# A new order of the opening, query sums on VectorE, and the shared group's sums on VectorE

## The chip, the cores and the metric

The kernel runs on one core of a Trainium2 chip. The metric is the device time of one execution in microseconds (us); lower is better. A core has a matrix engine (TensorE, PE in the profile), a vector engine (VectorE, DVE), a scalar engine (ScalarE, ACT), a general engine (GpSimd, POOL) and a queue engine that only issues transfers (SyncE, SP). Each engine takes its instructions in the order written, and waits on semaphores for the others.

## What is computed

The reference, cut to what matters (B, H, S, D of a head = 8, 8, 576, 64):

```python
# efficient attention, per batch and head
q_s = exp(q - max(q, axis=-1));  q_s = q_s / (sum(q_s, axis=-1) + 1e-9)   # over the 64 features
k_s = exp(k - max(k, axis=seq)); k_s = k_s / (sum(k_s, axis=seq) + 1e-9)  # over the 576 tokens
x = q_s @ (k_s^T @ v)                       # (8, 8, 576, 64), then heads side by side: (8, 576, 512)
# Fourier mix and channel block
u = x + real(fft(fft(x, axis=seq), axis=features))
un = (u - mean(u)) / sqrt(var(u) + 1e-6)
out = u + relu(un @ w_ch1) @ w_ch2          # 512 -> 2048 -> 512
```

All data are 32-bit floats, except that the two weights reach the device as 64-bit words, whose halves are turned into 32-bit floats there (`convert`).

## The kernel before

The eight batches are worked off as groups. For each batch the 576 tokens are taken as four tiles of 128 (A to D in the opening) and 64 left-over tokens; the left-over tokens of two batches share one tile `t`, whose results form an eighth group of 512 rows, the shared group. The groups run in the order 0 to 6, then the shared group, then 7 (`groups`). Group 0 uses plain products with the two weights (`plain`), converts the weights in passing (`convert`) and leaves seven Strassen combinations of their quarters in DRAM (`combine`, `deepen`). The later stages, numbered 1 to 8 by `order`, stream these and multiply by Strassen's scheme (`up`, `deep_down`), while attention and Fourier mix of the next batch go on beside them. Order 7 is the shared group's stage, with no attention beside it, and order 8 the last.

The order of all instructions is written out by hand: each step is a pair of a due time and a function; all pairs are sorted by time and called once, and the engines then follow this order. The due times set the order only, not the moment. The opening, which is all the work ahead of group 0's first up-projection, is a list of names and times in the string `OPENING`. In it:

- `loads_first` issues the loads. ScalarE's queue gets four loads of 32 rows of the shared tile (`shared`, L271); SP gets the four key loads (L281), two query loads of two tiles each (L290: A and B, then C and D), the values (L285, L286), the four first rows of the shared tile (`shared_firsts`, L274, which overwrite one row of each of ScalarE's four loads), tables, the second batch's keys and values, and the first weights (L347).
- `first_keys` turns keys to exponentials, transposes them (`turn`, `last`) and multiplies by the values (`kv`); `scale` writes the normalised matrix `kvr`.
- `q_exp_spread` gives the exponential of a query tile: a maximum on VectorE (`max`, L805), a subtraction (`less`, L810) on GpSimd, for the shared tile on VectorE, and an exponential on ScalarE (L814).
- `q_turn` transposes a query tile and copies it to a buffer `qT`, of which there are two.
- `q_times_kv` multiplies `qT` by a matrix of ones to get the sums of the exponentials (`ones`, L876), by `kvr` (`times`, L884), inverts the sums (`inverse`, L890 and L891) and scales the product on its way to the result tile `x` (`out`, L899). The shared tile takes its sums and scaling ahead of the transposition (`q_inverse`, L783 to L794, VectorE).
- `folded` adds and subtracts the four result tiles (`tokens`, L945) and folds columns, `block` and `mix_own` are the two steps of the Fourier transform, `norm` the statistics, scaling and transposition for the up-projection, whose first chunk is `half` (L1169) and whose others are `up` in `plain` (L1160).
- `c0` is the conversion of the first weight chunk; those of chunks 1 to 31 are placed by the list `words` behind the opening, whose end is the time `first`.

In `up`, `a_side` (L383 to L386) forms four sums of finished hidden blocks on the engine `e`. In `deep_down`, `a_step` (L1317) forms further sums, `into` (L1321) adds finished results to `x`, `sums` (L1324) adds results to each other; some of them run on the engine `E`. `plus` (L1378) adds a bank of products to an earlier one and so frees the bank for TensorE. For order 8, `e` and `E` are VectorE, otherwise GpSimd.

Results leave by `store`. Where rows have to be turned round (c not equal to u), the tile goes to DRAM (`mirror`, L1529) and from there in reversed order to the output (L1531). At the very end, `scatter` does it instead by an indirect store on GpSimd's queue (L1506) with a list of rows made by `iota`: once for half of a tile, once for a whole tile.

Of the kernel before, what the change touches and what calls it, by code (L numbers as in the profile page):

```python
# [40 lines left out]
F32 = mybir.dt.float32  # L41
I32, U32 = mybir.dt.int32, mybir.dt.uint32
# [4 lines left out]
P = 128  # L47
# [37 lines left out]
WARM = (3, 3), (24.7, 6), (41.9, 2), (43.45, 1), (44.5, 1)  # L85
OPENING = """
4.30 k00 max, 5.10 k00 exp, 5.50 k01 max, 6.05 k00 turn, 6.30 k01 exp, 6.65 k02 max, 7.06 k00 four,
7.25 k01 turn, 7.56 k02 exp, 7.75 k03 max, 8.32 k01 four, 8.51 k02 turn, 8.82 k03 exp, 8.90 A max, 9.50 B max,
9.58 k02 four, 9.65 A less, 9.77 k0 last, 10.10 k0 inverse, 10.27 k03 turn, 10.42 k0 fifth, 10.69 B less,
10.80 A exp, 11.20 k00 kv, 11.30 k03 four, 11.84 B exp, 11.85 A turn, 12.20 C max, 12.30 k01 kv, 12.45 A copy,  # L90
12.80 D max, 12.95 B turn, 12.95 C less, 13.40 A ones, 13.55 B copy, 13.99 D less, 14.10 C exp, 14.20 k02 kv,
14.35 A inverse, 14.85 C turn, 15.00 t max, 15.14 D exp, 15.30 k03 kv, 15.75 t less, 15.95 D turn,
16.35 k0 scale0, 16.40 B ones, 16.47 t exp, 16.80 k0 scale1, 17.14 t inverse, 17.25 B kv, 17.99 B inverse,
18.22 A kv, 18.35 C copy, 18.39 t normal, 19.01 B out, 19.19 t turn, 19.32 D copy, 19.63 k10 max, 19.69 C ones,
19.84 t copy, 20.30 A out, 20.43 k10 exp, 20.49 C kv, 20.92 C inverse, 21.39 t fold, 21.46 D ones,
22.09 t join, 22.26 D kv, 22.51 D inverse, 22.91 C out, 23.31 t kv, 23.53 D out, 24.15 tokens0, 24.21 k10 turn,
24.36 t parts, 24.77 tokens1, 25.39 columns0, 25.46 k10 four, 25.75 columns1, 26.23 by1, 26.59 by0,
26.80 c0 hi, 26.95 t folds, 27.45 c0 lo, 27.70 again0, 28.00 again1, 28.50 tokens3, 28.60 b0 times,
29.12 tokens2, 29.58 b1 times, 29.74 columns3, 29.80 b0 copies, 30.10 columns2, 30.56 b4 times, 30.58 by2,
30.78 b1 copies, 30.94 by3, 31.42 again2, 31.72 again3, 31.76 b4 copies, 32.22 k12 max, 32.32 b2 times,  # L100
32.89 c0 shift, 33.02 k12 exp, 33.30 b3 times, 33.59 c0 sign, 33.78 b2 copies, 34.19 k13 max, 34.28 k12 turn,
34.31 c0 add, 34.50 b3 copies, 34.86 k11 max, 35.05 k13 exp, 35.20 m0 times, 35.81 k12 four, 36.10 k13 turn,
36.31 m0 copy, 36.55 m1 times, 36.66 k11 exp, 36.81 m0 sums, 37.42 k13 four, 37.61 k1 last, 37.71 m0 add0,
37.92 m1 copy, 38.07 k11 turn, 38.27 k1 fifth, 38.39 m0 add1, 38.42 m1 sums, 38.77 k11 four, 38.92 k10 kv,
39.22 s00, 39.27 roots, 39.67 k11 kv, 39.69 m1 add1, 39.97 s01, 40.42 k12 kv, 40.87 root0, 40.99 m1 add0,
41.17 k13 kv, 41.67 scales0, 41.87 s11, 42.02 normal01, 42.62 s10, 42.77 turn01, 43.37 normal00, 43.52 root1,
43.87 scales1, 43.89 normal11, 43.95 laid01, 44.02 turn00, 44.22 normal10, 44.77 laid00, 44.87 turn10,
45.47 turn11, 45.62 laid10, 46.22 laid11, 53.00 k1 inverse, 53.30 k1 scale0, 53.60 k1 scale1"""
# [28 lines left out]
class _Block:  # L137
    def __init__(self, ctx, tc, q, kT, v, w1, w2, ft, cd, out):
# [38 lines left out]
        self.ones = c.tile([P, NR, H], F32, name="ones")  # L177
        nc.gpsimd.memset(self.ones[:], 0.0)
        for h in range(2):
            nc.gpsimd.memset(self.ones[64 * h:64 * h + 64].rearrange("p r h -> p (r h)")[:, h::H + 2], 1.0)  # L180

# [31 lines left out]
        self.unused = None  # L213
# [32 lines left out]
    def loads_first(self, fetch):  # L246
# [45 lines left out]
        def second(r):  # L292
# [6 lines left out]
        order = [lambda: nc.gpsimd.memset(v[0:64, 4, :], 0.0), shared, table, *(lambda r=r: keys(r) for r in range(NR)), lambda: queries(0),  # L299
                 lambda: values(0), lambda: queries(1), lambda: values(2), shared_firsts, self.tables,  # L300
# [214 lines left out]
    def first_keys(self, b):  # L515
# [4 lines left out]
        copy, box, top = nc.vector.tensor_copy if b == 0 else nc.scalar.copy, {}, {}  # L520
# [26 lines left out]
        def fifth():  # L547
            copy(self.fifth[64:], box["last"][64:])
# [26 lines left out]
    def opening(self, fetch, converted):  # L575
# [17 lines left out]
        named("t max,t less,t exp", self.q_exp_spread(shared, V))  # L593
        named("t inverse,t normal", self.q_inverse(shared, V, V))
# [3 lines left out]
        for n, it in own.items():  # L598
            named(f"{n} max,{n} less,{n} exp", self.q_exp_spread(it))
            named(f"{n} turn,{n} copy", self.q_turn(it))  # L600
            named(f"{n} ones,{n} kv,{n} inverse,{n} out", self.q_times_kv(it))
# [13 lines left out]
        for i in range(1):  # L615
            some = converted(i)
            named(f"c{i} hi,c{i} shift,c{i} sign,c{i} lo,c{i} add", some[:5])
            steps[f"c{i} add"] = lambda some=some: go(some[4:])
# [179 lines left out]
    def q_exp_spread(self, it, e=None):  # L798
# [9 lines left out]
        def less():  # L808
            m = live[it].pop()[:].unsqueeze(2).to_broadcast([P, H, DH])
            (e or nc.gpsimd).tensor_tensor(out=heads(), in0=heads(), in1=m, op=ALU.add)  # L810
# [14 lines left out]
    def q_turn(self, it):  # L825
# [3 lines left out]
        def copy():  # L829
            pt = box.pop()  # L830
            qT = self.work.tile([P, NR, P], F32, tag="qT", name="qT", bufs=2)
            self.nc.scalar.copy(qT[:], pt[:] if c == u else pt[:, :, ::-1])
# [34 lines left out]
    def q_times_kv(self, it):  # L867
# [3 lines left out]
        def ones():  # L871
# [813 lines left out]
```

## Time and profile before

| | us |
|---|---|
| median of 3 runs | 1072.61 (1072.57 to 1073.12) |
| profiled execution, its own time | 1072.76 |
| its span, first to last instruction | 1071.0 |
| TensorE busy | 1058.3 |
| VectorE busy | 685.9 |
| ScalarE busy | 404.8 |
| GpSimd busy | 422.5 |
| first up-projection product starts | 49.20 |
| last TensorE product ends | 1066.9 |

The granted TensorE clock is 0.999 over the span. The page gives the busy time of each engine, the span in slices, and the costliest groups of instructions by line, engine and operation, each with its count, its mean and the idle time ahead of it. In the timeline a row has start, duration, engine, line, operation, destination and source, shape, count, and in brackets how long the engine stood idle before and what released it. Rows of equal instructions in a run are merged: the duration is then that of all of them. A matrix product of 32-bit floats takes two passes on TensorE, and each pass is one MATMUL; a transposition takes one.

### The profile page before, as it was taken

The numbers are of one execution on the slowest core, as the hardware profiler recorded it, in microseconds if no ns is written. First come the engines' busy times: TensorE is split into PE (matmuls) and PEld (weight loads), VectorE is DVE, ScalarE is ACT, GpSimd is POOL, SyncE is SP. The second block draws the span as 40 slices with busy tenths as digits, with TensorE's granted clock in tenths as the row PEclk, the third lists the DMA queues.
The fourth block names the chain that finished last, engine by engine and source line by source line (L and its number), as shares of the span: only waits on it lengthen the run. The fifth ranks groups of instructions, "written<-read, shape, count | busy, mean of one in ns | idle before, by whom it ended". The sixth has DMA issues, their size and how long they took to land.

```text
span 1071.0 us, 16992 instructions
## 1 busy us (share of the span) xinstructions
PE 1058.3 (99%) x6394; PEld 922.4 (86%) x6394; DVE 685.9 (64%) x1317; ACT 404.8 (38%) x953; POOL 422.5 (39%) x352
## 2 busy tenths in 40 slices
PE   8999999999999999999999999999999999999998
PEld 7744556988898899889998999889988998899898
DVE  6897787684455874677556765687457742563563
ACT  5675534632245215521453234522552132131210
POOL 3262220265412743454515543374336353552000
PEclk9999999999999999999999999999999999999999
DMA  9486578648976576646755576547644674576464
GB/s 341 160 302 245 174 246 292 208 162 282 329 262 212 179 252 233 225 177 202 273 178 190 196 246 224 199 183 256 222 167 158 210 257 164 203 249 217 176 214 146
DMA packets 112933, 235.90 MB, mean 220 GB/s; under 512 B 22756, under 2 KB 74212, under 8 KB 102228
## 3 DMA queue, kind: packets, MB, share of 16 engines
q1 hardware_dynamic: 112244, 233.90, 63.8%
q8 instruction: 51, 0.84, 0.3%
q10 hardware_dynamic: 480, 0.52, 0.1%
q0 software_dynamic: 128, 0.39, 0.1%
q14 instruction: 30, 0.25, 0.1%
HBM read 199.66 MB, written 38.93 MB: 223 GB/s over the span
## 4 chain that ended last, share of the span: by engine, by line
PE 84%; DVE 3%; ACT 2%; issue 1%; POOL 1%; DMA 0%; POOLq 0%; DVEq 0%; ACTq 0%
PE bb L1244 15%; PE bb L1371 10%; PE bc L1244 10%; PE ba L1244 10%; PE bc L1371 6%; PE ba L1371 6%; PE bb L1341 4%; PE acc L716 2%; PE acc L884 2%; PE bc L1181 2%; PE bb L1460 2%; PE acc L997 2%; PE acc L1000 2%; PE acc L1025 2%; PE bc L1460 1%; PE ba L1460 1%
## 5 line engine op out<-in xcount | busy, mean ns | idle before, releaser
L1244 PE MATMUL bb<-unT,big 128*128 128x256 f32 x768 | 184.4, 380 | 0.8 <-DVE u L1214 0.8
L1244 PEld LDWEIGHTS bb<-unT,big 128*128 128x128 f32 x768 | 142.5, 190 | 20.3 <-DVE u L1214 2.3
L383 POOL TENSOR_TENSOR big<-big 128x512 f32<-128x512 f32 x28 | 35.9, 1281 | 255.9 <-ACT big L1256 255.9
L1256 ACT ACTIVATE big<-big 128x512 f32<-128x512 f32 x96 | 60.6, 631 | 194.9 <-DVE big L1255 194.5
L1244 PE MATMUL ba<-unT,big 128*128 128x256 f32 x512 | 123.8, 379 | 0.0
L1244 PE MATMUL bc<-unT,big 128*128 128x256 f32 x512 | 123.5, 380 | 0.0
L1214 DVE TENSOR_TENSOR u<-bb,s 128x512 f32<-128x512 f32 x66 | 45.6, 691 | 117.7 <-PE bb L1244 97.4
L1371 PE MATMUL bb<-big 128*128 128x128 f32 x848 | 105.2, 275 | 1.8 <-DVE u L1378 1.8
L1244 PEld LDWEIGHTS bc<-unT,big 128*128 128x128 f32 x512 | 94.7, 190 | 12.5 <-DVE big L1255 1.0
L1244 PEld LDWEIGHTS ba<-unT,big 128*128 128x128 f32 x512 | 94.4, 190 | 12.2 <-issue 0.5
L1371 PEld LDWEIGHTS bb<-big 128*128 128x128 f32 x848 | 99.6, 192 | 2.2 <-DVE u L1378 2.2
L1321 POOL TENSOR_TENSOR x<-x,big 128x512 f32<-128x512 f32 x45 | 57.7, 1297 | 62.7 <-issue 32.9
L1317 DVE TENSOR_TENSOR big<-big 128x512 f32<-128x512 f32 x94 | 78.1, 875 | 2.5 <-POOL big L386 2.5
L1371 PE MATMUL ba<-big 128*128 128x128 f32 x640 | 79.6, 275 | 0.0
L766 ACT ACTIVATE q<-q,qm 128x64 f32<-128x64 f32 x248 | 67.5, 342 | 31.2 <-DVE qm L760 25.9
L1371 PEld LDWEIGHTS ba<-big 128*128 128x128 f32 x640 | 76.3, 192 | 1.2
L1341 PE MATMUL bb<-big 128*128 128x256 f32 x256 | 58.7, 380 | 0.0
L1378 DVE TENSOR_TENSOR u<-bb,s 128x256 f32<-128x256 f32 x40 | 16.8, 421 | 64.6 <-PE bb L1371 59.9
L1255 DVE TENSOR_TENSOR big<-bc,u 128x512 f32<-128x512 f32 x64 | 44.0, 687 | 21.9 <-PE bc L1244 21.0
L1341 PEld LDWEIGHTS bb<-big 128*128 128x128 f32 x256 | 48.2, 190 | 8.0 <-DVE big L1255 1.1
L1371 PE MATMUL bc<-big 128*128 128x128 f32 x416 | 51.5, 275 | 0.0
L1371 PEld LDWEIGHTS bc<-big 128*128 128x128 f32 x416 | 48.9, 192 | 0.0
(265 smaller groups left out, 2014.8 us busy)
## 6 DMA issues: line engine op xcount, KB each, us to landing
big<-w2d SPq DMA_DIRECT2D x67, 1024.0 KB, 4.8
big<-w1s SPq DMA_DIRECT2D x64, 896.0 KB, 4.9
big<-w2s SPq DMA_DIRECT2D x16, 1024.0 KB, 6.4
big<-in_w_dram SPq DMA_DIRECT2D x21, 512.0 KB, 6.3
w2d<-big SPq DMA_DIRECT2D x42, 256.0 KB, 5.6
q<-in_q_dram SPq DMA_DIRECT2D x28, 256.0 KB, 6.4
k<-in_kT_dram SPq DMA_DIRECT2D x24, 288.0 KB, 5.6
v<-in_v_dram SPq DMA_DIRECT2D x24, 256.0 KB, 4.4
```

The lines of the kernel that those rows point to most:

```text
L383: e1.tensor_tensor(out=to(4), in0=at(2), in1=at(3), op=ALU.add)
L716: nc.tensor.matmul(pk, lhsT=ks[:, c, :], rhs=v[:, c, :], start=(c == 0), stop=(c == NC - 1))
L766: nc.scalar.activation(q[:, h, :], q[:, h, :], ACT.Exp, bias=m[:, h:h + 1])
L1214: plus = lambda t: V.tensor_tensor(out=temp(t), in0=box["bb"][:], in1=box["s1"][:], op=ALU.add)
L1244: nc.tensor.matmul(bank()[:, i, :], lhsT=w[:, WA_AT[m], k * P:(k + 1) * P], rhs=self.unT[g][:, B_AT[m], k, :], start=first and i == 0 and ...
L1255: steps = [(0, lambda: V.tensor_tensor(out=hp(i), in0=bank()[:], in1=u()[:], op=ALU.add)), (0.8, lambda: nc.scalar.activation(hp(i), hp(i) ...
L1256: (0.8, lambda: nc.scalar.activation(hp(i), hp(i), ACT.Relu))]
L1317: e.tensor_tensor(out=to(o), in0=to(x), in1=to(y), op=op)
L1321: E.tensor_tensor(out=x, in0=x, in1=tile(m), op=ALU.add)
L1341: nc.tensor.matmul(box[name][:, i, :], lhsT=h[p][:, A_AT[m], i * P:(i + 1) * P], rhs=self.stream[n][:, p, :], start=p == 0 and (m != 1 or ...
L1371: nc.tensor.matmul(box[place[n]][:, i, :], lhsT=own(m)(A_AT[n])[:, f, :], rhs=w[:, r // 2, r % 2 * P:r % 2 * P + P], start=first and f == ...
L1460: nc.tensor.matmul(bank()[:, i, :], lhsT=h[p][:, A_AT[m], i * P:(i + 1) * P], rhs=w[:, p, :], start=first and i == 0 and p == 0, stop=p == ...
```

## The change

The list `OPENING` is written anew, and with it:

- The sums of the four query tiles and of the shared tile are formed by VectorE (`reduce_sum`) as soon as the exponential is there, into one small tile `sums`; the matrix of ones and its products go. Two steps invert them, `inverse1` for the shared tile and C, `inverse2` for D, A and B.
- The shared tile, C and D are scaled on GpSimd ahead of their transposition; A and B are still scaled by VectorE on the way out of the product. C's and D's products are copied by ScalarE, and `tokens` reads them where they were formed.
- The shared tile's subtraction moves from VectorE to GpSimd, the fifth-row copy of the first keys (`fifth`) from VectorE to ScalarE.
- The transposed query tiles of batch 0 have a place each in the weight buffer `w1sb`, and three of the four products have a bank of their own.
- The load of the four first rows of the shared tile is issued ahead of the first query load.
- The second weight chunk's conversion (`c1`) moves into the opening; four warm-up products instead of three stand at its start; `first` is 47.6 instead of 46.9.
- `e` and `E` are VectorE for order 7 too.
- At the end the indirect store of half a tile becomes a store to DRAM and a mirrored one from there, both on SP.

```diff
-WARM = (3, 3), (24.7, 6), (41.9, 2), (43.45, 1), (44.5, 1)
+WARM = (3, 4), (23.6, 6), (42.1, 1), (43.9, 1)
...
-        order = [lambda: nc.gpsimd.memset(v[0:64, 4, :], 0.0), shared, table, *(lambda r=r: keys(r) for r in range(NR)), lambda: queries(0),
-                 lambda: values(0), lambda: queries(1), lambda: values(2), shared_firsts, self.tables,
+        order = [lambda: nc.gpsimd.memset(v[0:64, 4, :], 0.0), shared, table, *(lambda r=r: keys(r) for r in range(NR)), shared_firsts, lambda: queries(0),
+                 lambda: values(0), lambda: queries(1), lambda: values(2), self.tables,
...
-            copy(self.fifth[64:], box["last"][64:])
+            nc.scalar.copy(self.fifth[64:], box["last"][64:])
...
-        named("t max,t less,t exp", self.q_exp_spread(shared, V))
-        named("t inverse,t normal", self.q_inverse(shared, V, V))
+        named("t max,t less,t exp", self.q_exp_spread(shared))
+        sums = self.small.tile([P, 5, H], F32, tag="sums", name="sums", bufs=1)
+        firsts = {"t": shared, **{n: own[n] for n in "CDAB"}}
+        heads = {n: self.live[it][0].rearrange("p (h d) -> p h d", h=H) for n, it in firsts.items()}
+        spread = {n: sums[:, i].unsqueeze(2).to_broadcast([P, H, DH]) for i, n in enumerate(firsts)}
+        for i, n in enumerate(firsts):
+            steps[f"{n} sum"] = lambda i=i, n=n: V.reduce_sum(sums[:, i], heads[n], axis=AX.X)
+            if n in "tCD":
+                steps[f"{n} normal"] = lambda n=n: G.tensor_tensor(out=heads[n], in0=heads[n], in1=spread[n], op=ALU.mult)
+            else:
+                self.live[own[n]].append(spread[n])
+
+        def inverse(s):
+            V.tensor_scalar(out=sums[:, s], in0=sums[:, s], scalar1=ATT_EPS, scalar2=None, op0=ALU.add)
+            V.reciprocal(sums[:, s], sums[:, s])
+
+        for i, s in enumerate((slice(0, 2), slice(2, 5))):
+            steps[f"inverse{i + 1}"] = lambda s=s: inverse(s)
...
-            named(f"{n} ones,{n} kv,{n} inverse,{n} out", self.q_times_kv(it))
+            named(f"{n} kv,{n} out", self.q_times_kv(it))
...
-        for i in range(1):
+        for i in range(2):
             some = converted(i)
...
-            qT = self.work.tile([P, NR, P], F32, tag="qT", name="qT", bufs=2)
-            self.nc.scalar.copy(qT[:], pt[:] if c == u else pt[:, :, ::-1])
+            if b == 0:
+                qT = self.w1sb[:, 1 + c + 2 * u, :].rearrange("p (r n) -> p r n", n=P)
+            else:
+                qT = self.work.tile([P, NR, P], F32, tag="qT", name="qT", bufs=2)[:]
+            self.nc.scalar.copy(qT, pt[:] if c == u else pt[:, :, ::-1])
...
-            px = self.acc((P, D))
-            box.insert(0, px)
+            if b == 0 and (c, u) != (1, 0):
+                n = {(0, 0): "bb", (1, 1): "bc", (0, 1): "ba"}[c, u]
+                t = self.ps.tile([P, 512], F32, tag=n, name=n)
+                px = t[:]
+            else:
+                px = self.acc((P, D))
+            box.append(px)
             box.extend(rec)
+            if b == 0 and c != u and not rec:
+                self.px[c, u] = px
...
-        base, e = self.base[order], V if order == B else nc.gpsimd
+        base, e = self.base[order], V if order >= B - 1 else nc.gpsimd
...
-        E = V if last else G
+        E = V if order >= B - 1 else G
...
-            steps.extend(self.scatter(t - 8 + 3.1, g, 1, 0, lambda: self.xs[g, 0][:, 1, HD:], 1))
+            half(t - 8 + 3.1, 1, 0, 1, 3)
...
-    first, second, both = 46.9, 56, 77
+    first, second, both = 47.6, 56, 77
...
-    words = [first + 0.3, first + 1.4, *(first + 0.9 + 1.7 * i for i in range(1, NF - 2))]
+    words = [first + 0.7, *(first + 0.9 + 1.7 * i for i in range(1, NF - 2))]
...
-    for i, dt in enumerate(words, 1):
+    for i, dt in enumerate(words, 2):
```

## The prediction

> **What bounds the kernel now.** First the page's busy line, then the table of busy time by stretch (us, TensorE, its weight loads, VectorE, ScalarE, GpSimd, each with its number of instructions, then granted clock, DMA share, GB/s).
>
> ```profile
> PE 1058.3 (99%) x6394; PEld 922.4 (86%) x6394; DVE 685.9 (64%) x1317; ACT 404.8 (38%) x953; POOL 422.5 (39%) x352
> ```
> ```profile
> 0.00:24.00 24.00, 20.83 (x139) 18.55 (x140) 14.29 (x32) 13.54 (x26) 9.53 (x29) 1.00 0.98 336
> 24.00:49.20 25.20, 23.21 (x167) 20.63 (x167) 22.35 (x59) 15.10 (x40) 5.02 (x6) 1.00 0.62 213
> 876.00:972.00 96.00, 94.41 (x607) 87.61 (x607) 45.19 (x67) 22.96 (x39) 46.71 (x35) 1.00 0.63 218
> ```
>
> From 49.2 us on TensorE has hardly a pause, and the order and number of its products stay the same there. So only three places can change the time: when TensorE starts the first up-projection, the 1.6 us that it loses in the seventh stage (876 to 972), and what follows its last product. I read these three in the timeline, with the landing times of loads and stores beside it. The opening:
>
> ```profile
> 3.60 0.39 SPq L290 DMA_DIRECT2D big<-in_q_dram  x1
> 7.30 0.62 SPq L274 DMA_DIRECT2D big<-in_q_dram  x1
> 8.65 1.28 DVE L805 TENSOR_REDUCE qm<-big 128x8 f32<-128x512 f32 x2 [0.50 <-DMA big<-in_q_dram]
> 9.48 2.04 POOL L810 TENSOR_TENSOR big<-big,qm 128x512 f32<-128x512 f32 x2 [4.17 <-DVE qm L805]
> 26.14 1.28 DVE L945 TENSOR_TENSOR eo<-x 128x512 f32<-128x512 f32 x2
> 49.20 3.62 PE L1169 MATMUL ba<-unT,big 128*128 128x256 f32 x16
> 53.02 3.70 PE L1160 MATMUL bb<-unT,big 128*128 128x512 f32 x8 [0.19 <-POOL big L377]
> ```
>
> Read: the first query load is issued at 3.60 and releases VectorE's first query maximum at 8.65; the four-row load of the shared tile (L274) stands behind six larger loads; the first up-projection starts at 49.20, and the second chunk waits for GpSimd to finish its weight. The seventh stage:
>
> ```profile
> 926.13 1.58 POOL L383 TENSOR_TENSOR big<-big 128x512 f32<-128x512 f32 x1 [6.90 <-ACT big L1256]
> 931.14 1.26 POOL L386 TENSOR_TENSOR big<-big 128x512 f32<-128x512 f32 x1
> 932.44 5.68 DVE L1317 TENSOR_TENSOR big<-big 128x512 f32<-128x512 f32 x4 [2.50 <-POOL big L386]
> 938.04 0.41 DVE L1378 TENSOR_TENSOR u<-bb,s 128x256 f32<-128x256 f32 x1
> 938.51 2.05 PE L1371 MATMUL bb<-big 128*128 128x128 f32 x16 [1.59 <-DVE u L1378]
> ```
>
> Read: four sums on GpSimd end at 932.4, VectorE's next sums wait for the last of them, the bank's release (L1378) stands behind these, and TensorE waits 1.59. The end:
>
> ```profile
> 1061.27 6.45 SPq L1522 DMA_DIRECT2D out_dram<-x  x2
> 1063.49 1.17 POOL L1506 DMA_INDIRECT out_dram<-x,row  x1 [86.18 <-DMA out_dram<-x]
> 1066.92 0.97 POOL L1506 DMA_INDIRECT out_dram<-x,row  x1 [2.26 <-DMA out_dram<-x,row]
> 1066.93 0.42 DVE L1352 TENSOR_TENSOR x<-bb,x 128x256 f32<-128x256 f32 x1 [3.03 <-PE bb L1341]
> ```
>
> Read: the second indirect store has its data at 1063.90, but waits until the first has landed (1066.10). It lands itself at 1069.90, the last of all; SP's last plain store, issued at 1067.38, lands at 1068.96. The span ends at 1071.0.
>
> **The opening, part by part.** Gone: 16 products with ones (32 passes at 0.11, 3.6 us of TensorE), four pairs of add and reciprocal (0.17 + 0.20 each), two VectorE scalings of products (0.68 each), and VectorE's subtraction, scaling (0.69, 0.64) and fifth-row copy (0.69). New: four more VectorE sums (row L783, 0.69 alone, 0.61 in a run), two inverses for all (0.4 each), three GpSimd scalings, one more GpSimd subtraction (1.04, row L810), two ScalarE copies (0.59). The second weight's conversion (0.64 + 0.67 ScalarE, 0.68 + 0.69 VectorE, 1.30 GpSimd) moves from after 49.2 into the opening. A GpSimd multiply with a spread operand is in no row: nearest is the add with one, 1.04; the other bound is the plain add, 1.30 (L377). I take 1.04.
>
> One move runs against the rest. The four-row load overwrites rows of the four 64 KB loads on ScalarE's queue, so in the built order of instructions it waits for all of them; the last is issued at 2.14 and lands at 7.04. In its old place this was over. Now it stands on SP ahead of both query loads and all values: SP stands still until 7.07, needs 0.62 for it, and issues the first query load at 7.72 instead of 3.60. The transfers before it are done by 7.30, so it starts on empty queues. A 512 KB load issued alone at 38.30 landed at 41.77, 3.47 later; so 7.72 + 3.47 = 11.19 instead of 8.63. Bounds: 8.63 (no loss) and 11.7 (a start 0.5 worse). What follows keeps its distances: second query load 11.49 to 14.05, last values 13.35 to 15.9, first weight 24.46 to 27.0.
>
> From there I laid down the built order of each queue, each instruction with its row's duration, starting when its engine is free and what it waits for is done. The kernel before laid down in this way starts the two projections at 49.14 and 52.85 (rows 49.20 and 53.02), so differences are good to some 0.2 us. The new chain: first maximum 11.22; C's maximum 14.08 (second query load); two maxima and four sums at 0.61, inverse 0.4: 18.29; three GpSimd scalings from 18.33 to 21.34; on TensorE t's turn 19.42, A's product 20.09, the turns of C and D, products B, D, C, and t's product ending at 25.45 (row before: 26.39). First token sum 24.5 (26.14); first transform product 30.2 (31.10); first statistics 39.8 (41.90). Most of this lead goes again: VectorE now does the other half's sums and additions (0.41 + 0.41 + 0.15 + 0.41 + 0.64) after the first statistics, not ahead of them, so the first scale comes at 44.0 (44.15) and the first projection at 48.86. The second chunk no longer waits for its weight: 52.30 against 52.85, a gain of **0.55**. By the same method: 8.63 for the query load gives 50.20 (gain 2.65), 11.7 gives 52.5 (0.3), and GpSimd at 1.30 costs 0.72.
>
> TensorE's speed is a further bound. Passes of 128 columns start 0.21 us apart until 11.6, after 3.3 us without a gap, and 0.11 apart from then on. In the new order it works from 8.44 to 11.32 and then waits for the values until 12.83. A pause of 2.07 us at 29.04 left the passes at 0.12, so I take them as fast; if they start slow again for 3.3 us, the first projection comes 0.95 later (49.81).
>
> The Trainium skill ("TensorE: Matmul & The Clock Gate", Part 1) says that the full clock needs a busy window of about 3.4 us, and that these windows run freely. This speaks against the new order, whose run is shorter than that; it would have the later case unless the warm-up products, four now for three, count, and the total below would be some 1 us higher.
>
> **The seventh stage.** 16 side sums, 6 combination sums and 11 additions to results go from GpSimd (1.26 to 1.59 here) to VectorE (0.69 in the eighth stage, L383): 33 x 0.69 = 22.8 us on top of 45.2 in 96. What is behind them there is the release of banks. The last side sums then end near 929 instead of 932.4, VectorE has done its combination sums by about 934.4, and the release is ready when TensorE reaches it at 935.3: the 1.59 falls away. I take **1.6**. In the eighth stage, where these sums are on VectorE, the same loop shows one lengthened start of 0.1, so the bounds are a gain of 1.75 and of 1.2.
>
> **The end.** One indirect store goes, so the other need not wait: its data is there at 1063.90, it starts 0.9 later and lands 3.0 after that, near 1067.8. In its stead come a store to DRAM (issue 1062.6, 1.65 to land) and a mirrored store behind it on SP, some 1064.6, 512 pieces of 256 bytes. Such a one behind a 1 MB load took 6.2 to land; its own part was about 3. It should land near 1068.5, ahead of the last plain store at 1068.96, which now ends: 1069.90 - 1068.96 = **0.9**. If it delays that store, which shares its queue, the gain falls to nothing, or turns into a loss of 0.5.
>
> **Sum.** 0.55 + 1.6 + 0.9 = 3.05 off the profiled run of 1072.76 (span 1071.0 and 1.76 around it): 1069.7. The median of the runs shown is 0.15 lower; I say 1069.7.
>
> **Rivals.** (1) The load loses nothing: it would need a landing near 8.6. For: it is small, and ScalarE's loads may land sooner without the query load beside them. Against: SP takes its instructions in order, and the query load came behind the four key loads in before too. 1069.7 - 2.1 = 1067.6; chance 0.08. (2) The opening gives nothing, by slow passes or GpSimd at 1.30, and may lose 0.4 to 1.1: 1070.4 to 1071.3; chance 0.25. (3) The change doesn't do what it says in the seventh stage: VectorE, with 68 of 96 us, releases banks just as late. For: VectorE's queue is in order. Against: the eighth stage. 1069.7 + 1.6 = 1071.3; chance 0.09. (4) Slower: the stalled load queue starves the opening. The first projection follows the query load at up to 1 us per us, so it decides from a landing at 11.2 + 3.05 + 2.15 = 16.4; that needs a transfer of 8 us, which no row of a lone load has. At 17 it gives 1075.5; chance 0.05. The forecast, 1069.0 to 1070.4, has 0.53.
>
> **How the numbers follow.** 0.2% is 2.1 us, about what a measurement of this kernel tells from no change: faster means under 1070.5, slower over 1074.8. Faster: 0.53, 0.08 and a small part of (2), 0.65. Slower: 0.05 and a rest for what I overlook, 0.08. Same: 0.27. The range takes in the forecast, (2), (3) and part of (1): 1068.3 to 1071.8.
>
> **What would show it.** Right: SP's four-row load at about 7.1 and the first query load at 7.7; A's maximum near 11.2; first projection near 48.9 with no wait behind it; no TensorE wait near 937; one indirect store at about 1064.8. Wrong: a maximum at 8.7 or after 12.5, passes of 0.21 after 12.8, TensorE waiting for L1378's counterpart in the seventh stage, or a last landing of the mirrored store after 1068.

## The result, and the profile after

| | before | changed |
|---|---|---|
| median, us | 1072.61 (9 runs, 1071.82 to 1074.87) | 1075.41 (9 runs, 1073.52 to 1077.55) |
| ratio to before | | 1.0023, 95% interval 1.0014 to 1.0031 |
| span of the profiled execution | 1071.0 | 1073.0 |

The kernel became slower by 0.23%; the forecast was 1069.7, with 1068.3 to 1071.8 as its range. The profiled execution, at 1074.76, is one of the quicker ones: its span is 2.0 longer than that of the profile before, while the medians differ by 2.8. First the same two views as before the change: the busy line of the page, and the table of busy time by stretch (us, then TensorE, its weight loads, VectorE, ScalarE, GpSimd, each with its number of instructions, then granted clock, DMA share, GB/s), both of the changed kernel.

```profile
PE 1054.7 (98%) x6360; PEld 917.9 (86%) x6360; DVE 699.4 (65%) x1343; ACT 405.4 (38%) x956; POOL 380.6 (35%) x318
```
```profile
0.00:24.00 24.00, 16.18 (x96) 13.32 (x97) 13.52 (x26) 12.18 (x24) 13.43 (x30) 0.93 0.86 264
24.00:49.20 25.20, 22.91 (x168) 20.70 (x166) 23.64 (x60) 18.29 (x46) 6.69 (x7) 1.00 0.94 302
876.00:972.00 96.00, 96.00 (x623) 89.17 (x622) 58.03 (x99) 23.48 (x41) 7.39 (x6) 1.00 0.63 221
```

Read the last row first: in the seventh stage TensorE is now busy for all 96.00 (94.41 before), VectorE has 58.03 instead of 45.19, GpSimd 7.39 instead of 46.71. That part did what it was meant to do. The first row holds the loss: in the first 24 us the loads run at 264 GB/s instead of 336, and TensorE is busy for 16.18 instead of 20.83, though the products with ones account for some 3.1 of the difference (28 of their 32 passes, 0.11 each, fell into this stretch).

Where the 2.0 us of the span come from is read by setting the starts of the same TensorE products side by side (worked out from the two traces; the order of products is the same from the first up-projection on):

| product | before | changed | later by |
|---|---|---|---|
| first up-projection | 49.20 | 51.47 | 2.27 |
| second chunk | 53.02 | 55.00 | 1.98 |
| query product of the next group | 105.06 | 107.21 | 2.15 |
| the one after it | 110.90 | 114.25 | 3.35 |
| turn of group 1's first tile | 162.82 | 167.03 | 4.21 |
| seventh stage, ahead of the old wait | 893.63 | 898.07 | 4.44 |
| behind the old wait | 938.51 | 941.20 | 2.69 |
| last product | 1066.51 | 1068.97 | 2.46 |
| end of the span | 1071.0 | 1073.0 | 2.0 |

So the opening loses 1.98 where 0.55 was to be won; another 2.5 go behind the opening, where nothing was forecast; the seventh stage gives back 1.75, stretches without a lasting wait 0.2, the end 0.46. The opening in the timeline of the changed kernel:

```profile
7.44 0.69 SPq L270 DMA_DIRECT2D big<-in_q_dram  x1
8.18 0.39 SPq L286 DMA_DIRECT2D big<-in_q_dram  x1
12.03 1.28 DVE L817 TENSOR_REDUCE qm<-big 128x8 f32<-128x512 f32 x2 [3.63 <-DMA big<-in_q_dram]
...
19.94 3.04 POOL L597 TENSOR_TENSOR big<-big,sums 128x512 f32<-128x512 f32 x3 [1.49 <-ACT big L847]
20.37 0.64 DVE L602 TENSOR_SCALAR sums<-sums 128x24 f32<-128x24 f32 x1
26.75 0.69 DVE L955 TENSOR_TENSOR eo<-acc,x 128x512 f32<-128x512 f32 x1 [0.68 <-ACT x L909]
51.47 3.69 PE L1179 MATMUL ba<-unT,big 128*128 128x256 f32 x16 [0.72 <-ACT unT L1124]
```

The four-row load (L270) is issued at 7.44, the first query load (L286) at 8.18 instead of 3.60, and VectorE's first maximum comes at 12.03 instead of 8.65. From there each step is late, and the lead that the new order was to win (the first token sum, L955, at 24.5 for 26.14) never appears: 26.75. What the stop on SP does to the loads is seen in stretches of 4 us, first of the kernel before, then of the changed one:

```profile
4.00:8.00 4.00, 3.46 (x11) 1.84 (x10) 2.87 (x4) 2.97 (x7) 1.20 (x7) 1.00 1.03 342
8.00:12.00 4.00, 3.71 (x19) 3.49 (x20) 3.40 (x7) 3.43 (x9) 2.04 (x2) 1.00 1.06 382
```
```profile
4.00:8.00 4.00, 3.03 (x13) 1.88 (x12) 2.62 (x4) 2.39 (x6) 0.93 (x3) 1.00 0.73 213
8.00:12.00 4.00, 2.91 (x12) 2.29 (x12) 0.40 (x1) 3.37 (x9) 0.00 (x0) 0.58 0.66 188
```

The last column is GB/s. 342 - 213 and 382 - 188 over 4 us each are 1.3 MB that were not moved; at the 382 of the kernel before that is 3.4 us of transfers, and the first query load lands at 12.0 instead of 8.63, 3.4 later. In the second of the two stretches VectorE is busy for 0.40 (3.40 before) and GpSimd not at all (2.04 before).

Behind the opening, TensorE's two longest waits of the changed kernel that the kernel before does not have, or has shorter, and what stands ahead of them on VectorE and ScalarE:

```profile
57.69 0.68 DVE L365 TENSOR_SCALAR big<-acc 128x512 int32<-128x512 int32 x1
...
58.29 1.04 DVE L547 TENSOR_SCALAR kinv<-kinv 128x4 f32<-128x4 f32 x1
59.92 0.67 DVE L368 SCALAR_TENSOR_TENSOR big<-acc,big 128x512 int32<-128x512 int32 x1
60.62 0.64 ACT L371 ACTIVATE acc<-big 128x512 f32<-128x512 f32 x1 [1.00 <-DVE big L368]
...
114.25 1.16 PE L899 MATMUL acc<-kvr,qT 128*128 128x128 f32 x8 [1.09 <-ACT qT L847]
...
167.03 0.65 PE L1115 MATMUL tr<-ident,eo 128*128 128x128 f32 x4 [0.71 <-ACT eo L1109]
```

A weight conversion is a pair on VectorE, L365 and L368, and ScalarE's next one (L371) needs the buffer that L368 frees. In the kernel before, the second keys' inverse and scaling stood between two such pairs; here L547 to L559 stand inside one, so L368 starts at 59.92, 2.2 after its partner, and ScalarE stands idle for 1.00. One of these steps, L547, works on 128x4 numbers and yet takes 1.04. In all thirteen profiles of this document this step of the second keys ends 0.02 to 0.03 behind a GpSimd instruction that began before it (here 59.33, behind L373's 59.30), so what it takes depends on when it starts: 0.22 in the kernel before, 1.04 here. The chain of conversions, which is 2.33 late at 56.36 (54.03 before), is 3.37 late at 60.62 (57.25). ScalarE's part of it catches up at times, to 1.9, but VectorE's stays 3.0 to 3.5 late up to 110, while TensorE is only 2.0 late. At 110.9 the kernel before had no slack in this chain (ScalarE's copy ends at 110.84, the product starts at 110.90), so TensorE waits for the difference.

The seventh stage and the end, in the changed kernel:

```profile
939.72 0.42 DVE L1388 TENSOR_TENSOR u<-bb,s 128x256 f32<-128x256 f32 x1
941.20 1.95 PE L1381 MATMUL bb<-big 128*128 128x128 f32 x16
```
```profile
1066.91 0.67 SPq L1540 DMA_DIRECT2D out_dram<-mirror  x1
1067.28 1.20 POOL L1515 DMA_INDIRECT out_dram<-x,row  x1 [105.05 <-DMA out_dram<-x]
1069.39 0.42 DVE L1362 TENSOR_TENSOR x<-bb,x 128x256 f32<-128x256 f32 x1 [3.03 <-PE bb L1351]
1069.84 0.34 SPq L1531 DMA_DIRECT2D out_dram<-x  x1
```

The bank's release (L1388) ends at 940.14, 1.06 ahead of the product that needs it, which has no bracket, so no wait. At the end there is one indirect store; the three stores that are under way together land at 1070.92 (mirrored), 1071.56 (indirect, 4.28 after its issue; 2.61 and 2.98 before) and 1071.89 (the last plain one, 2.05 after its issue; 1.73 before).

### The profile page after: what moved, and what is told of

Its sections match the earlier page's. It is cut to its first block, busy times and chain, and to the rows that moved or that the text cites. A ratio compares the mean times of both kernels' runs of the same rounds, so it can differ in the third digit from the quotient of the medians.

```text
span 1073.0 us, 16919 instructions
## 1 busy us (share of the span) xinstructions
PE 1054.7 (98%) x6360; PEld 917.9 (86%) x6360; DVE 699.4 (65%) x1343; ACT 405.4 (38%) x956; POOL 380.6 (35%) x318
## 4 chain that ended last, share of the span: by engine, by line
PE 84%; DVE 3%; ACT 2%; DMA 1%; issue 0%; DVEq 0%; ACTq 0%
PE bb L1254 15%; PE bb L1381 10%; PE bc L1254 10%; PE ba L1254 10%; PE bc L1381 6%; PE ba L1381 6%; PE bb L1351 5%; PE acc L728 2%; PE acc L899 2%; PE bb L1470 2%; PE acc L1007 2%; PE acc L1010 2%; PE bc L1191 2%; PE acc L1035 1%; PE bc L1470 1%; PE ba L1470 1%
## 5 line engine op out<-in xcount | busy, mean ns | idle before, releaser
L379 POOL TENSOR_TENSOR big<-big 128x512 f32<-128x512 f32 x24 | 30.5, 1269 | 225.5 <-ACT big L1266 225.5
L1327 DVE TENSOR_TENSOR big<-big 128x512 f32<-128x512 f32 x98 | 76.3, 818 | 0.0
L1388 DVE TENSOR_TENSOR u<-bb,s 128x256 f32<-128x256 f32 x40 | 16.9, 421 | 63.9 <-PE bb L1381 60.6
L1130 POOL TENSOR_TENSOR unT<-unT 128x512 f32<-128x512 f32 x8 | 14.1, 1763 | 123.8 <-DVE unT L1130 123.8
```

Source lines behind the costliest of these rows:

```text
L379: e1.tensor_tensor(out=to(4), in0=at(2), in1=at(3), op=ALU.add)
L1327: e.tensor_tensor(out=to(o), in0=to(x), in1=to(y), op=op)
```

## The experiments

Times are ratios to the kernel before, run beside each on the same chip in five rounds; its median there was 1073.0 to 1073.5. One caution holds for all: one profile shows one execution, and even the old opening does not always take the same time. The second chunk starts at 53.02, 52.97 and 52.76 in three profiles of kernels with the old opening (before, the seventh stage alone, both with the end), but at 55.18 in a fourth (the end alone). There the first query load landed at 9.67 (8.63 before), and TensorE's passes stayed 0.21 apart until 14.9 instead of 11.6. So single rows that differ by up to 2 us between two profiles show little by themselves, and a verdict rests on rows and times together.

**The wait alone, in the kernel before.**

```diff
-  ..., *(keys), queries(0), values(0), queries(1), values(2), shared_firsts, tables
+  ..., *(keys), shared_firsts, queries(0), values(0), queries(1), values(2), tables
```

> The kernel before, with one difference: the four-row load of the shared tile is put where the change has it, behind the key loads and ahead of the query loads, where it has to wait for the four loads on ScalarE's queue. Nothing else of the change. Theory A: SP issues it at about 7.1 to 7.4, the first query load at 7.8 to 8.2 (3.60 before), the first query maximum comes at 11.2 to 12.0 (8.65 before), the loads behind it 3.4 to 6 late; the first up-projection comes 2.5 to 4.5 after 49.20; time 1075 to 1077. Rival B (the order of vector work is what costs): the queries land late, but the kernel before has slack for it; first projection within 1 us of 49.20, time 1072.6 to 1073.6.

Measured: 1.0036 (1.0022 to 1.0050), 1077.04. Its opening:

```profile
7.59 0.71 SPq L274 DMA_DIRECT2D big<-in_q_dram  x1
8.35 0.39 SPq L290 DMA_DIRECT2D big<-in_q_dram  x1
...
12.04 1.28 DVE L805 TENSOR_REDUCE qm<-big 128x8 f32<-128x512 f32 x2 [3.48 <-DMA big<-in_q_dram]
...
53.52 3.62 PE L1169 MATMUL ba<-unT,big 128*128 128x256 f32 x16
```

With nothing else of the change, the same rows appear: 7.59, 8.35, 12.04, and the first up-projection is 4.32 late. This one line costs as much as the whole change does, or more (1.0036 against 1.0023; the intervals overlap). Theory A holds, B falls: the kernel before has no slack for it.

**Taking the reason for the wait away.** The loads on ScalarE's queue leave out the rows that the four-row load writes.

```diff
-                nc.scalar.dma_start(tail[i * Q:(i + 1) * Q], flat[a:a + Q])
+                nc.scalar.dma_start(tail[i * Q + 1:(i + 1) * Q], flat[a + 1:a + Q])
```

> The changed kernel, with one difference: the four loads of the shared tile on ScalarE's queue leave out the four first rows that the four-row load writes, so that load has nothing to wait for but its own queue. Theory A (SP standing behind the four loads delays the whole load stream, and with it everything): the four-row load is issued near 4.0 instead of 7.44, the first query load near 4.7 instead of 8.18, VectorE's first query maximum comes at 9 to 10 instead of 12.03; the first up-projection moves from 51.47 to between 47.8 and 49.0, the second chunk from 55.00 to between 51.3 and 52.5; time 1075.4 less some 3.2 = 1072.2, and if the two losses behind the opening (1.4 by 114, 0.9 by 167) go with the late loads, as low as 1070. Rival B (the new order of sums and scalings on VectorE and GpSimd costs the time, whatever the loads do): the queries land early all the same, the first projection stays after 50.5, time 1074.4 to 1075.4. Rival C (the losses by 114 and 167 come from where steps of the second keys now stand between conversions on VectorE): projection as in A, but both losses stay, time 1072 to 1072.5.

Measured: 1.0078 (1.0064 to 1.0092), 1081.97, slower still. The rows say why:

```profile
7.12 0.69 SPq L270 DMA_DIRECT2D big<-in_q_dram  x1
7.86 0.39 SPq L286 DMA_DIRECT2D big<-in_q_dram  x1
11.71 0.38 SPq L281 DMA_DIRECT2D big<-in_v_dram  x1
...
15.92 0.38 SPq L286 DMA_DIRECT2D big<-in_q_dram  x1
...
19.85 0.48 SPq L282 DMA_DIRECT2D big<-in_v_dram  x1
```

Loads of 31 rows instead of 32 land at 7.10, 11.69, 15.90 and 19.83: some 4.2 us for 62 KB each, one behind the other, 15 GB/s. Each load of the opening waits for the one issued eight before it, ScalarE's among them, so SP stops at 7.12, 11.71, 15.92 and 19.85, each time just behind such a landing. The Trainium skill ("DMA: Bandwidth & Descriptors", "Why a DMA increments its semaphore by 16 and not by 1") says that a transfer is spread over the largest number of engines up to 16 that divides the outer size of both of its sides. For 31 rows that is one engine, and this run agrees: 4.2 us for 62 KB, where the 64 KB loads of 32 rows land 0.9 to 1.4 apart. The experiment thus didn't take the wait away, but made it longer. It still speaks for A: the first weight lands 5.5 later than in the changed kernel, and the first up-projection comes at 58.65, 7.2 later. TensorE's clock was granted at 0.5 from 8.6 to 25.7 in this run, which may be a part of it.

**The four-row load on GpSimd's queue.**

```diff
-            load(tail[0:P:Q], ...)
+            nc.gpsimd.dma_start(tail[0:P:Q], ...)
```

> The changed kernel, with one difference: the four-row load of the shared tile is issued by GpSimd, which has nothing to do from 5 to 12.8, so it waits there and SP goes on. Theory A (SP standing still until 7.4 delays the load stream, and by it the opening): SP issues the first query load at 3.6 to 4.0 as in the kernel before, the first query maximum comes at 8.7 to 9.3 (12.03 in the changed kernel), the first weight lands at 24.5 to 26 (30.19); GpSimd issues its load at 7.1 to 7.6; the first up-projection comes at 47.5 to 48.8 (51.47); time 1075.4 - 3.2 = 1072.2 if the losses by 114 and 167 stay, 1070 if these too came from late loads. Rival B (VectorE's and GpSimd's new work sets the opening): loads early, first projection still after 50.5, time 1074.4 or more. Rival D (a load issued by GpSimd lands late and holds up the shared tile, which stands second on VectorE's queue): loads early, second maximum after 11.5, projection 49 to 50.5, time 1073 to 1074.4.

Measured: 1.0020 (1.0008 to 1.0033), 1075.51: nothing won.

```profile
4.11 0.39 SPq L286 DMA_DIRECT2D big<-in_q_dram  x1
8.23 0.80 POOL L270 DMA_DIRECT2D big<-in_q_dram  x1 [3.30 <-DMA big<-in_q_dram]
9.18 0.69 DVE L817 TENSOR_REDUCE qm<-big 128x8 f32<-128x512 f32 x1 [0.57 <-DMA big<-in_q_dram]
13.94 0.69 DVE L817 TENSOR_REDUCE qm<-big 128x8 f32<-128x512 f32 x1 [4.07 <-DMA big<-in_q_dram]
17.50 0.66 PE L834 MATMUL tr<-ident,big 128*128 128x128 f32 x4 [3.86 <-ACT big L826]
```

SP goes on at 4.11, and the first maximum comes at 9.18. But 8 KB that are asked for among full queues are there only at 13.9, 5.7 after the issue (2.0 on the empty queues of the changed kernel), and the shared tile's maximum is second on VectorE, so all stands behind it for 4.07. The first up-projection starts at 52.76, 1.3 later than in the changed kernel; TensorE's clock was granted at 0.5 from 18.3 to 21.7, where its passes are 0.21 apart, which may have a part in this. Theory A's 47.5 to 48.8 is missed. By these two numbers, 52.76 and 1075.51, this would be rival B; D forecast 49 to 50.5 and 1073 to 1074.4. The rows show D's mechanism, at a higher price, and whether B holds beside it is left to the run with the shared tile last. This one shows the other half of the matter: the new order needs these four rows early, and the old place gives them late.

**The second keys' steps, between two conversions again.**

```diff
-  53.00 k1 inverse, 53.30 k1 scale0, 53.60 k1 scale1
+  53.70 k1 inverse, 54.00 k1 scale0, 54.30 k1 scale1
```

> The changed kernel, with one difference: the three steps of the second keys (inverse and two scalings, on VectorE) are due 0.7 later, as much as the first layer was moved by the change, so they stand between two weight conversions again and not inside one. Theory C (in the changed kernel they hold a conversion up by 1.0 at 58.3 to 59.9, ScalarE's next conversion waits 1.00 for it at 60.62, and the chain of conversions carries this to the products at 114 and 167): ScalarE's wait near 60.6 is gone, TensorE's waits of 1.09 at 114.24 and of 0.71 at 167.03 shrink to 0.3 or less together with the rest, time 1075.4 - 1.0 to 1.8 = 1073.6 to 1074.4. Theory A alone (these losses come from loads that are late): both waits stay within 0.3, time 1075.2 to 1075.6.

Measured: 1.0009 (1.0000 to 1.0018), 1074.38. On VectorE, ScalarE and TensorE:

```profile
58.40 0.69 DVE L368 SCALAR_TENSOR_TENSOR big<-acc,big 128x512 int32<-128x512 int32 x1
59.01 0.31 DVE L547 TENSOR_SCALAR kinv<-kinv 128x4 f32<-128x4 f32 x1
59.52 0.64 ACT L371 ACTIVATE acc<-big 128x512 f32<-128x512 f32 x1
...
112.97 1.16 PE L899 MATMUL acc<-kvr,qT 128*128 128x128 f32 x8 [0.24 <-ACT qT L847]
...
165.41 0.66 PE L1115 MATMUL tr<-ident,eo 128*128 128x128 f32 x4 [0.36 <-ACT eo L1109]
```

L368 comes ahead of L547, ScalarE goes on at 59.52 without its wait, and the waits fall from 1.09 to 0.24 and from 0.71 to 0.36. The opening is the same (51.47), the last product 1.67 earlier. By the times alone (1.0009 against 1.0023) the intervals overlap; with the rows, theory C holds for most of the losses behind the opening.

**Both mendings together.** The four-row load by GpSimd and the second keys' steps 0.7 later.

> The changed kernel with both differences: the four-row load by GpSimd and the three steps of the second keys due 0.7 later. If A holds for the opening and C for the losses behind it, their gains add: first projection at 47.5 to 48.8, no wait over 0.4 near 111 and 164, time 1075.4 - 3.2 - 1.4 = 1070.8, with a low end at 1069; that would be some 2 below the kernel before. If one of the two theories falls, 1072 to 1074.

Measured: 1.0009 (1.0000 to 1.0019), 1074.74, above both forecasts. The first up-projection is as late as with GpSimd's load alone (52.77), and TensorE waits 1.04 near 115 and 0.86 near 168 though ScalarE's wait near 60.6 is gone. ScalarE now stands idle for 1.99 ahead of 79.69, behind VectorE (L368); the same conversion waits 0.73 in the kernel before, 1.83 in the changed one and 1.16 with the second keys' steps later alone. So C explains most of the changed kernel's loss behind the opening, but is not the only way in which this chain falls behind; what holds it up here was not followed further.

**Something under way while SP stands.** With the second keys' steps 0.7 later as well:

```diff
-  *(keys), shared_firsts, queries(0), values(0), queries(1), values(2)
+  *(keys), queries(0), shared_firsts, values(0), queries(1), values(2)      (first)
+  *(keys), queries(0), queries(1), shared_firsts, values(0), values(2)      (second)
```

> The kernel with the second keys' steps due 0.7 later (k1_later, 1074.4), and the four-row load moved behind the first query load. SP stands still as long as before (until the last of ScalarE's four loads has landed, 7.1 to 7.5), but a 512 KB transfer is on its way meanwhile. Theory A (what costs is that nothing is on its way while SP stands): first query load issued at 3.6 to 4.1, first query maximum at 8.8 to 9.3 (12.03), four rows there at 9.5 to 10.5, so the shared tile's maximum is not held up; the later loads 1.5 to 2.5 earlier than in the changed kernel; first up-projection at 49.0 to 50.0 instead of 51.47; time 1074.4 - 1.6 to 2.4 = 1072.0 to 1072.8. Rival B (vector work sets the opening): projection after 50.8, 1073.9 or more. Rival D (four rows among other transfers land late, as with GpSimd, where it took 5.7): second maximum after 11.5, projection after 50.5.

> As query_first, but the four-row load stands behind both query loads and ahead of the values, so 1 MB is on its way while SP stands. Theory A: first query maximum at 8.8 to 9.3, second query load landed at 10.3 to 11 (15.55 in the changed kernel), four rows at 10 to 12, first values at 12 to 13 (13.5 to 13.8), later loads 3 earlier than in the changed kernel; first up-projection at 48.4 to 49.7, time 1074.4 - 1.8 to 3.1 = 1071.3 to 1072.6. Rival D (the four rows land only behind the 1 MB and later, after 12.5, and VectorE's queue, where the shared tile's maximum is second, stands until then): projection at 50 to 51.5, time 1073 to 1074.4.

Measured: 0.9999 (0.9990 to 1.0007), 1073.06, and 0.9988 (0.9979 to 0.9996), 1072.13. The second one's rows:

```profile
3.83 0.90 SPq L286 DMA_DIRECT2D big<-in_q_dram  x2
7.49 0.69 SPq L270 DMA_DIRECT2D big<-in_q_dram  x1
...
10.63 0.69 DVE L817 TENSOR_REDUCE qm<-big 128x8 f32<-128x512 f32 x1 [0.81 <-DMA big<-in_q_dram]
...
50.31 3.69 PE L1179 MATMUL ba<-unT,big 128*128 128x256 f32 x16 [0.72 <-ACT unT L1124]
```

SP stands still just as long (7.49), but 1 MB is under way: 336 and 320 GB/s in the stretches from 4 to 8 and 8 to 12, where the changed kernel has 213 and 188. The four rows land at 10.61. The first variant has half of that cover: the loads behind its stop come only 0.1 to 1.3 earlier than in the changed kernel (the first weight at 30.11 for 30.19), where A gave 1.5 to 2.5, and its first up-projection at 51.00 misses the 49.0 to 50.0. The times come in the order of the cover, 1.0009 (no cover, second keys' steps later), 0.9999, 0.9988, which is what A says; the intervals of neighbours overlap, those of the first and the last do not. The second variant's 50.31 is 0.6 beyond its range too; its passes are 0.21 apart from 9.8 to 16.3, with the clock granted at 0.5 from 9.5 to 16.3, which the expectation left out.

**The old place of the load, and the shared tile last.** Its steps come last of the five tiles on every engine; the rest of the new opening stays, and the second keys' steps are 0.7 later.

> As k1_later, with the four-row load where the kernel before had it, behind queries and values, and the shared tile's steps (maximum, subtraction, exponential, sum, scaling, turn, fold) last of the five tiles on every engine instead of second; all other parts of the new opening stay: sums on VectorE, scalings on GpSimd, no products with ones. Theory A (the late loads are the cost, the new vector work isn't): loads as in the kernel before, first maximum at 8.7 to 9.3, four rows at 13.4 to 14.5, first up-projection at 48.5 to 49.7, so within 0.7 of the kernel before (49.20), time 1074.4 - 2.4 = 1072.0 (1071.4 to 1072.8). Rival B (sums on VectorE and scalings on GpSimd lengthen the chain by more than the products with ones did): projection after 50.5 in spite of the early loads, time 1073.4 or more.

Measured: 0.9988 (0.9979 to 0.9996), 1072.50.

```profile
3.91 0.39 SPq L286 DMA_DIRECT2D big<-in_q_dram  x1
...
8.15 0.62 SPq L270 DMA_DIRECT2D big<-in_q_dram  x1
9.29 0.69 DVE L817 TENSOR_REDUCE qm<-big 128x8 f32<-128x512 f32 x1 [0.54 <-DMA big<-in_q_dram]
...
49.68 3.69 PE L1179 MATMUL ba<-unT,big 128*128 128x256 f32 x16 [0.72 <-ACT unT L1124]
```

The first up-projection starts at 49.68, 0.5 behind the kernel before, the second chunk at 53.21, 0.2 behind. Theory A, within its range; rival B falls: in this order sums on VectorE and scalings on GpSimd cost about what the products with ones cost, as far as one execution of each tells. The run changes two things at once, the place of the load and that of the shared tile, and the share of each was not measured.

**The seventh stage alone, the end alone, and both, with the old opening.** The edits are the two lines on `e` and `E`, and the line that replaces the second `scatter`.

> The kernel before, with only the seventh stage's sums (side sums, combination sums, additions to results) on VectorE. If these sums on GpSimd held up the bank's release near 937: TensorE's wait of 1.59 at 938.51 is gone, time 1072.6 - 1.7 = 1070.9. Rival (the wait goes only because the whole kernel is shifted, or VectorE releases banks late in another place): a wait of 0.5 or more elsewhere between 876 and 972, time 1072 to 1072.6.

> The kernel before, with only the end changed: the second indirect store replaced by a store to DRAM and a mirrored store from there on SP. As the changed kernel's trace has it (3.2 from the last addition's end to the end of the span, against 3.65), time 1072.6 - 0.45 = 1072.2: the last plain store lands 2.05 after its issue instead of 1.58. If the stores did not hinder each other, as forecast, 1072.6 - 0.9 = 1071.7. Rival (no gain, the mirrored store holds up the others as much as the second indirect store did): 1072.6 or more.

> The kernel before, with the seventh stage's sums on VectorE and the changed end, and the old opening. If the parts add, time is that of the seventh stage alone (0.9984 of before, 1.7 less) less some 0.45 by the end: 1070.9 against 1073.0. If the end gains nothing by the time, as the run with it alone would allow (1.0002 of before): 1071.3. The changed kernel less this one is then the cost of the new opening with all it carries behind it: 4 to 4.5.

Measured: 0.9984 (0.9975 to 0.9993), 1071.20; 1.0002 (0.9993 to 1.0011), 1073.58; 0.9986 (0.9978 to 0.9995), 1072.25. The first is as expected, 0.0016 x 1073 = 1.7, and TensorE goes from product to product at the old place of the wait:

```profile
934.64 1.95 PE L1371 MATMUL bc<-big,unT 128*128 128x128 f32 x16
934.96 0.41 DVE L1378 TENSOR_TENSOR u<-bb,s 128x256 f32<-128x256 f32 x1
...
936.43 1.84 PE L1371 MATMUL bb<-big 128*128 128x128 f32 x15
```

The end alone is inconclusive by its time: from the start of the last product to the end of the span it takes 4.03 against 4.46, a gain of 0.43, but its time can't tell that from nothing. Nor can the run with both: 0.9986 against 0.9984, each with 0.0009 to either side.

## Why the prediction was wrong

The forecast was 3.05 less, the profiled span came out 2.0 longer. Of the 5.05 between them the opening has 2.5 (0.55 to be won, 1.98 lost), the stretch behind it 2.5, the end 0.4; the seventh stage and the rest gave 0.4 more than forecast.

- **SP stops for the four loads.** Right as a mechanism: four-row load forecast at 7.07, first query load at 7.72. Measured 7.44 and 8.18, since the last of the four loads landed at 7.36 in this execution (7.04 before). The query load then took 3.83 instead of the 3.47 assumed and landed at 12.01, behind the prediction's bound of 11.7.
- **"What follows keeps its distances."** This is the step that failed in the opening. It moved all later loads by 2.56, the delay of the first query load. The query load was 3.38 late, the second one 4.06, the last values 4.37, the first weight 5.73 (30.19), so the second query load came at 15.55, not at 14.05. An idle stretch of the queue is lost for all that is behind it, and here the loads also ran 7% slower (a weight chunk every 1.50 instead of 1.40). That is not the stop's doing: the weight chunks are issued 1.46 apart in all eight kernels with the new opening, also where the load is in its old place, and 1.32 apart in all five with the old one, the one with the wait alone among them; why was not found. With the landing times of the changed kernel, the same laying down of queues gives 50.36 for the first projection instead of 48.86, an estimate, by which the loads are 1.5 of the error of 2.6. With the loads early again and the shared tile last it was measured at 49.68, 1.8 of the 2.6. That the load stream is the place is shown by the wait alone (4 us), by the cover (2 us back) and by the shared tile last (49.68).
- **Durations in the new order.** What remains, some 1, was not taken apart. Rows priced alone are a part of it: `inverse2` was put at 0.4; L602 takes 0.64 and L603 0.30 beside GpSimd's scalings, and L602 ends at 21.01, just behind the first of them (20.98).
- **"From 49.2 us on TensorE has hardly a pause, and the order and number of its products stay the same there."** True of TensorE, false as a reason for looking at three places only. The order on VectorE did change: `first` moved by 0.7 and the second keys' due times, 53.00 to 53.60, did not. This is the second step that failed, a term that the prediction put at nothing. The loss behind the opening is 2.5 by the trace; mending the due times gave 1.7 at the last product and 0.0014 of the time, and the rest of it stays open.
- **TensorE's speed.** In the changed kernel the passes were 0.11 apart at 6.2 to 7.7, 0.21 apart from 9.1 to 11.3 (the clock granted at 0.5 from 8.63 to 12.04), and 0.11 apart from 13.8 on, as taken. It was not a safe step: behind the wait of 2.79 in the run with the wait alone they stayed slow from 13.88 to 17.24.
- **GpSimd's multiply with a spread operand** at 1.04: three take 3.04. Right.
- **The seventh stage**, 1.6 forecast: 1.75 in the trace, 1.7 in time. Right, for the reason given: the release ends 1.06 ahead of the product. But VectorE's busy time rose by 12.8, not by the 22.8 of the sum. The sum left out that VectorE's own sums become shorter without GpSimd's beside them: L1317's 128x512 sums took 1.10 in the mean (1.42 in the four that start at 932.44), its counterpart L1327's take 0.74. And TensorE reached the bank at 936.9 in the kernel before (938.51 less its wait of 1.59), not at 935.3, which leaves more room.
- **The end**, 0.9 forecast: the mechanism was right, the size not. One indirect store at 1064.8 in old times (1067.28 - 2.46), the mirrored store at 1068.5 (1070.92 - 2.46). But the last plain store took 2.05 and lands 0.47 after the time assumed, so 0.46 is left. A part of this is a misread row: the sixteen semaphore increments of this store came from 1068.95 to 1069.11 in the kernel before, so it had landed at 1069.11, 1.73 after its issue, and not at 1068.96; 0.8 was to be won. The other 0.3 fits the stated possibility that stores on one queue delay each other, but which of the two stores beside it delayed it was not tested. The sign "a last landing of the mirrored store after 1068" contradicts the prediction's own 1068.5.
- **The rivals.** The fourth, a starved load queue, was given 1075.5 and 0.05, with the condition that the first query load lands behind 16.4. Its mechanism came true with a landing at 12.0: the condition was worked out from one load's landing and without the losses behind the opening, the 2.5. That its 1075.5 is so near the 1075.41 measured is luck, since half of the loss came from another place.

The new opening as built, with the conversions behind it, costs 1.0023 - 0.9986 = 0.0037, some 4 us; with the loads covered, or the shared tile last, it is level with the old one: 0.9988 in both against 0.9986. These and the seventh stage alone (0.9984) beat both kernels, and can't be told from each other.

## What to carry to other kernels

A transfer that must wait belongs behind transfers that can run, not ahead of them: here it cost the bytes that nobody asked for meanwhile, and everything behind it in the stream was late by that much or more. When an opening or any block of steps is moved in a plan of due times, look for steps that kept their old times: they now fall into other gaps. And price small operations by the rows beside which they will stand, not by the rows that ran alone.

## What was not expected of the hardware

- A load of 31 rows of 2 KB takes 4.2 us and holds up the next; loads of 32 rows land 0.9 to 1.4 after each other in the changed kernel (3.96, 5.35, 6.25, 7.36), with a key load between them.
- An 8 KB load takes 2.0 us on empty queues (7.44 to 9.47), 3.1 behind 1 MB (7.49 to 10.61), 5.7 from GpSimd's queue among full ones (8.23 to 13.9).
- A VectorE operation on 128x4 numbers takes 1.04 at 58.29, where the same step takes 0.22 in the kernel before, and ends with GpSimd's 128x512 instruction (59.33; GpSimd's L373 starts at 58.00 and takes 1.30). It ends 0.02 to 0.03 behind a GpSimd instruction in every profile here.
- TensorE's passes change from fast to slow without a long pause: in the second cover variant they are 0.11 apart until 9.5 and 0.21 apart from 9.8 on, with granted clock 0.69 in the stretch from 8 to 12; waits of 0.60 and 1.09 lie shortly ahead (at 7.27 and 9.02), and TensorE was busy for 1.72 of the 3.41 from 6.10 to 9.51. The table in Part 1 of the Trainium skill ("TensorE: Matmul & The Clock Gate") ties the slow clock to an idle window of about 3.4 us; further on, the same Part tells of a kernel that falls back by frequent short idle times. The waits here are shorter than that window, and the passes became slow all the same. No run shows where the limit lies: in the first cover variant TensorE was busy for 1.69 of 3.41 from 15.47 on, and the clock stayed at 1.00.
